# Sliding-window attention with an MLP block: three-engine W1 casts, PV heads in another order, paced casts and respaced tail steps

## Chip, cores, metric

The kernel runs on one core of one Trainium2 chip. The metric is the device time of one launch in microseconds (us); lower is better. A profiled execution has a time of its own, and inside it a span from the first to the last instruction; all places in time below are counted from the start of that span.

## What is computed

Causal attention with a window of 64 keys, 8 batches of 8 heads, 576 tokens, head size 64; the heads side by side are x, which goes through a layer norm and a two-layer MLP with ReLU, and is added to its result. Inputs and output are float32.

```python
scores = (1 / sqrt(64)) * q @ k.T
mask = (rel >= 0) & (rel < 64)          # rel = query position - key position
attn = softmax(where(mask, scores, -1e9))
x = attn @ v                            # (8, 576, 512)
xn = (x - mean(x)) / sqrt(var(x) + 1e-6) * g_ln
out = x + relu(xn @ w_ch1) @ w_ch2      # 512 -> 2048 -> 512
```

## The kernel before, in words

**Groups and periods.** The 8 x 576 token rows are cut into nine groups of 512 rows: group g below 8 holds tokens 0 to 511 of batch g, group 8 holds the last 64 tokens ("tails") of all eight batches. The loop `for g in range(NGRP)` (L639) runs the MLP of group g as a list of units of TensorE work (`mlp_units`, L400), and between the units it places the attention of the next group: `at(i, f, ...)` puts a step in the slot behind unit i. I call the stretch of one g "period g". Everything is written out in this order by hand; each engine then takes its own instructions strictly in that order and waits on semaphores, so a step that waits holds up all that stands behind it on its engine.

**Attention of a batch.** Its tokens are four blocks of 128 queries (kb or j from 0 to 3; a block is two windows of 64). `load_qk`, `load_v` (L73, L140) issue loads on SP's queue. `cast_q`, `cast_v` (L123, L149) make float16 of them on GpSimd (POOL). For batches 0 to 3 `t_main` (L217) transposes q and k on TensorE (PE) and copies from PSUM to `qkT` on ScalarE (ACT) or VectorE (DVE); later batches use DMA transposes. `vA` holds v by blocks and `vB` the same shifted by 64 tokens; for batches 0 and 1 `vB` is cast piece by piece (`vB_cur`, `vB_prev`, L161, L164), later `make_vB` (L167) makes it by two DMAs that POOL issues. `v32`, the float32 v, has one buffer, so batch b+1's v load waits for all readers of batch b's. `s_mm` (L253) is the scores and their exponentials on ACT (two instructions, even heads first, then odd ones), `s_mask` (L291) multiplies by the mask on DVE (batches 0 and 1 have the mask added on PE instead), `b_step` (L298) is attn @ v ("PV") per head on PE, then on DVE the division by the sum (`rcp`, `xn`) and the statistics; `r_step` (L325) is 1/std on ACT, `z_step` (L334) normalizes on DVE, `zt_step` (L350) transposes on PE and copies to `zT` on ACT. `bz(i, ...)` puts b_step, r_step and z_step in slots i, i+1, i+2.

**MLP.** Layer 1 is 16 column blocks of the 2048 hidden units, each four matmuls of 512 rows (`l1`, L405) or, in period 0 in part and in period 1 throughout, of two halves of 256 rows (`l1_half`, L435); ACT applies ReLU into `hrT`. Period 0 has a plain layer 2: `l2_two` (L448) for the first two blocks, `l2` (L416) for the others, and `add_out` (L427) adds on DVE into `osb1` (two buffers) and sends a store on POOL's queue. From period 1 on layer 2 is a Strassen-Winograd scheme of seven half-size products (`product`, L465, 14 units; `post`, L489, adds them up on DVE), with sums of `hrT` made on DVE in every period (`presum`, L390) and differences of W2 made once (`t_weights`, L373, eight DVE instructions over all; tiles `tw`, and one kind in `w2s` itself). The PSUM pool of layer 1 and of `l2` has two banks, so a unit waits for the sum of the tile two before it.

**Weights.** W1 comes in eight loads of 512 KB, the last four into the space of `w2s`; a load i holds two 128-row chunks c. `w1_cast` (L187) scales chunk c by g_ln and casts: c = 0 on POOL, all eight ahead of batch 1's casts, c = 1 on ACT, each at a place of its own. `rest_of_loads` (L616) then issues, in slot 6 of period 0, W2's casts and later loads, the second half of batch 1's loads and casts, and batch 2's q and k loads.

**Pacing.** POOL casts compete in time with DVE. `pace(t)` (L347) is a one-column POOL copy of a tile: it does nothing but make POOL wait for that tile, and so places the cast behind it. In the kernel before only batches 4 and later and the tails are paced.

**Tails.** `TAILS` (L629) gives the slots of periods 6 and 7 for the tail group's loads, casts, scores (first argument 8 for s_mm, then the block), masks, PV and transposes. `keep_clock(n)` (L563) issues n matmuls of no use to keep PE's clock up at the start.

Of the kernel before, what the change touches and what calls it, by code (L numbers as in the profile page):

```python
# [18 lines left out]
def kernel(  # L19
# [141 lines left out]
    def vB_cur(b, c, eng):  # L161
        evac(eng, vB[b][64:128, c, :, 0:D], v32[b][0:64, c])
# [21 lines left out]
            .rearrange("(c p) n -> p c n", p=128),  # L184
        )

    def w1_cast(i, c):  # L187
        q2, pr = divmod(i, 2)
        t = wst[("w1", i)]
        kc = 2 * pr + c  # L190
        dst = w1g[:, kc, (HID // 4) * q2:(HID // 4) * (q2 + 1)]
        if c == 0:
            nc.gpsimd.tensor_scalar(out=dst, in0=t[:, c], scalar1=g4[:, kc:kc + 1], scalar2=None, op0=ALU.mult)
        else:
            nc.scalar.activation(out=dst, in_=t[:, c], func=AF.Identity, bias=0.0, scale=g4[:, kc:kc + 1])

    def w2_load(i):
        t = p_wst.tile([128, 2, DM], FP32, tag="wld", name=f"w2s_{i}")
# [99 lines left out]
    def b_step(g, kb):  # L298
        kblk = f"{g}_{kb}"
        if kb % 2 == 0:  # L300
            x_norm[(g, kb // 2)] = p_xn.tile([128, 2, H, D], FP32, tag="xn", name=f"xn_{kblk}")
        xn = x_norm[(g, kb // 2)][:, kb % 2]
        xps = ps_x.tile([128, H, 128], FP32, tag="xps", name=f"xps_{kblk}")
        pt = pts.pop((g, kb))
        for h in range(H):
            par, hp = h % 2, h // 2
            for r in range(2):
                if g == NGRP - 1:
                    rhs = vT[kb][:, r, h, :]
                else:  # L310
                    rhs = (vA if r else vB)[g][:, kb, h, :]
                nc.tensor.matmul(out=xps[64 * r:64 * r + 64, h, :D + 1], lhsT=pt[:, par, hp, r, :], rhs=rhs,  # L312
                                 start=True, stop=True)
        rcp = p_blk.tile([128, H], FP32, tag="rcp", name=f"rcp_{kblk}")
        nc.vector.reciprocal(out=rcp, in_=xps[:, :, D])  # L315
        rcp_b = bass.AP(tensor=rcp.tensor, offset=rcp[:, :].offset,
                        ap=[rcp[:, :].ap[0], rcp[:, :].ap[1], [0, D]])
        nc.vector.tensor_tensor(out=xn, in0=xps[:, :, 0:D], in1=rcp_b, op=ALU.mult)  # L318
        stats = p_blk.tile([128, nc.vector.BN_STATS_DIM], FP32, tag="stats", name=f"stats_{kblk}")
        nc.vector.bn_stats(out=stats, in_=xn.rearrange("p h d -> p (h d)"))  # L320
        mv = p_blk.tile([128, 2], FP32, tag="mv", name=f"mv_{kblk}", bufs=5)
        nc.vector.bn_aggr(out=mv, in_=stats)  # L322
        mvs[(g, kb)] = mv
# [76 lines left out]
    def mlp_units(g, split=0, two=False):  # L400
# [64 lines left out]
        def product(n, t):  # L465
            bank, first = {1: ("X", 1), 2: ("Y", 1), 6: ("X", 0), 5: ("Z", 1), 7: ("X", 0), 3: ("Z", 0), 4: ("X", 0)}[n]
            if first and t == 0:
                pool, tag = (ps_t, "tp") if bank == "X" else (ps_mm, "mm")
                xyz[bank] = pool.tile([128, 2, 256], FP32, tag=tag, name=f"w{bank}_{g}")
            w1, w2 = slice(0, 8), slice(8, 16)  # L470
            for hc in range(8):
                tok = slice(128 * t, 128 * t + 128)
                tok2 = slice(256 + 128 * t, 256 + 128 * t + 128)
                lhsT = {1: lambda: hrT[:, hc, tok], 2: lambda: hrT[:, 8 + hc, tok], 3: lambda: sw[4][:, hc, tok],
                        4: lambda: hrT[:, 8 + hc, tok2], 5: lambda: sw[1][:, hc, tok],
                        6: lambda: sw[2][:, hc, tok], 7: lambda: sw[3][:, hc, tok]}[n]()
                rhs = {1: lambda: w2s[:, hc, lo], 2: lambda: w2s[:, 8 + hc, lo], 3: lambda: w2s[:, 8 + hc, hi],
                       4: lambda: tw[4][:, hc], 5: lambda: tw[1][:, hc], 6: lambda: tw[2][:, hc],
                       7: lambda: w2s[:, hc, hi]}[n]()
                nc.tensor.matmul(out=xyz[bank][:, t], lhsT=lhsT, rhs=rhs, start=bool(first and t == 0 and hc == 0),  # L480
                                 stop=(t == 1 and hc == 7), skip_group_check=True)
            if last and n == 4:
                post(n, slice(t, t + 1))
            elif t == 1:
                post(n, slice(0, 2))

        last = g == NGRP - 1
# [67 lines left out]
    cast_qk(0, 1)  # L555
    cast_v(0, 2, 3)
    cast_v(0, 3, 4)
    for i in range(8):
        w1_cast(i, 0)

    warm = ps_mm.tile([128, 512], FP32, tag="mm", name="warm")

    def keep_clock(n):  # L563
        m = mbias[:, :]
        mb = bass.AP(tensor=m.tensor, offset=m.offset, ap=[m.ap[0], [0, 8], m.ap[1]])
        for _ in range(n):
            nc.tensor.matmul(out=warm[:, :].rearrange("p (a i) -> p a i", i=64), lhsT=ident16, rhs=mb,
                             start=True, stop=True)


    keep_clock(4)
    keep_clock(1)
    t_main(0, 0, 0)
    keep_clock(2)
    t_main(0, 1, 0)
# [17 lines left out]
    z_step(0, 1)  # L593
    keep_clock(2)
    vB_prev(0, 2, 0)
    w1_cast(0, 1)
    s_mm(0, 2, True)
    zt_step(0, 0)
    b_step(0, 2)
    z_step(0, 2)  # L600
    zt_step(0, 1)
    w1_cast(1, 1)
    vB_cur(0, 3, 0)
    s_mm(0, 3, True)
    w1_cast(2, 1)
    w1_cast(3, 1)


    load_qk(1, 0)
# [6 lines left out]
    def rest_of_loads():  # L616
        for i in range(8):
# [9 lines left out]
        load_qk(2, 1)  # L627

    TAILS = {  # L629
        6: ((0, load_tail, 0), (3, cast_tail, 0), (7, x_tail, 0), (11, s_mm, 8, 0), (12, s_mask, 8, 0),  # L630
            (17, b_step, 8, 0), (23, zt_step, 8, 0),
            (9, load_tail, 1), (12, cast_tail, 1), (16, x_tail, 1), (20, load_tail, 2), (24, cast_tail, 2),
            (28, x_tail, 2)),
        7: ((0, s_mm, 8, 1), (1, s_mask, 8, 1), (6, b_step, 8, 1), (12, zt_step, 8, 1),
# [4 lines left out]
    for g in range(NGRP):  # L639
# [12 lines left out]
        if g == 0:  # L652
            at(0, b_step, 0, 3)
            at(0, z_step, 0, 3)
            for j in range(4):
                at(3 + j, w1_cast, 4 + j, 1)
                at(10 + j, r_step, 0, j)
            at(6, rest_of_loads)
            at(1, zt_step, 0, 2)
            at(3, zt_step, 0, 3)  # L660
            at(11, t_main, 1, 0, 0, 1)
            at(12, t_main, 1, 1, 0, 1)
            at(13, vB_cur, 1, 0, 1)
            at(13, vB_prev, 1, 0, 1)
            at(13, vB_cur, 1, 1, 1)
            at(13, vB_prev, 1, 1, 1)
            at(16, s_mm, 1, 0, True)
            at(17, s_mm, 1, 1, True)
            bz(18, 1, 0)
            bz(21, 1, 1)  # L670
            at(22, zt_step, 1, 0)
            at(24, zt_step, 1, 1)
            at(26, t_main, 1, 0, 1, 0)
            at(27, t_main, 1, 1, 1, 1)
            at(28, vB_cur, 1, 2, 0)
            at(28, vB_prev, 1, 2, 1)
            at(29, vB_cur, 1, 3, 0)
            at(29, s_mm, 1, 2, True)
            at(30, s_mm, 1, 3, True)
            at(30, load_v, 2, 0, 4)  # L680
            at(30, cast_qk, 2, 0)
            at(30, cast_qk, 2, 1)
            bz(31, 1, 2)
        if g == 1:
            at(0, alloc_qkT, 2)
            bz(1, 1, 3)
            at(2, zt_step, 1, 2)
            at(5, zt_step, 1, 3)
            at(4, alloc_v, 2)
            at(4, alloc_vB, 2)  # L690
            at(5, cast_v, 2, 0, 4)
            at(5, make_vB, 2)
            at(2, t_main, 2, 0, 0, 1)
            at(3, t_main, 2, 1, 0, 0)
            at(4, t_main, 2, 0, 1, 1)
            at(6, t_main, 2, 1, 1, 0)
            at(18, t_main, 3, 0, 0, 0)
            at(20, t_main, 3, 1, 0, 0)
            at(24, t_main, 3, 0, 1, 0)
            at(26, t_main, 3, 1, 1, 0)  # L700
            for j in range(4):
                at(9 + 4 * j, s_mm, 2, j)
                at(10 + 4 * j, s_mask, 2, j)
                bz(13 + 4 * j, 2, j)
                at(17 + 4 * j, zt_step, 2, j)
        if g > 0:
            if g == 1:
                for n, i in enumerate((1, 2, 4, 3)):
                    for c in range(2):
                        at(1 + 2 * n + c, t_weights, i, c)  # L710
            for u, i, c in ((10, 3, 0), (12, 3, 1), (14, 1, 0), (14, 2, 0), (15, 4, 0), (16, 1, 1), (17, 2, 1), (18, 4, 1)) if g == 1 else (
                    (6, 3, 0), (10, 3, 1), (12, 1, 0), (13, 2, 0), (14, 4, 0), (16, 1, 1), (17, 2, 1), (18, 4, 1)):
                at(u, presum, g, i, c)
# [19 lines left out]
        if 0 < g and b + 1 < B:  # L733
# [3 lines left out]
            at(e + 1, load_qk, n, 1)  # L737
            at(e + 4, load_v, n, 0, 4)
            if n < NPE:
                at(e + 8, cast_qk, n, 0)  # L740
                at(e + 8, alloc_qkT, n)
                at(e + 10, cast_qk, n, 1)
                at(e + 16, alloc_v, n)
                at(e + 16, cast_v, n, 0, 4)
                at(e + 16, alloc_vB, n)
                at(e + 16, make_vB, n)
            else:
                at(3, alloc_qkT, n)
                for u, x, half in ((3, 0, 0), (5, 1, 0), (8, 0, 1), (10, 1, 1)):
# [48 lines left out]
```

The softmax here doesn't subtract the row's maximum and nothing guards it: scores larger than these inputs give would overflow.

## Time and profile before

| | us |
|---|---|
| median of 4 runs | 330.19 |
| lowest and highest | 328.62, 331.68 |
| profiled execution | 330.18 |
| its span | 328.5 |
| PE busy in the span | 302.6 |
| DVE, ACT, POOL busy | 204.1, 174.9, 128.0 |

The matmuls of layer 1 start at these times, by period:

| period | 0 | 1 | 2 | 3 | 4 | 5 | 6 | 7 | 8 |
|---|---|---|---|---|---|---|---|---|---|
| start, us | 21.62 | 62.96 | 107.66 | 138.74 | 169.71 | 200.68 | 231.65 | 266.58 | 296.62 |

How to read the lines of a profile: a timeline line is start, duration, engine, line of the kernel, operation, output tile <- input tiles, shape, count, and in square brackets the idle time of the engine before it and what ended that. Names such as `qkT` or `tw` leave out buffer numbers. A busy PE includes the drain of its last matmul, so the lengths of neighbouring groups overlap a little. PEclk is the share of TensorE's full clock that was granted. DMA share is the mean busy share of the 16 DMA engines; it passes 1 where packets overlap.

### The profile page before, as it was taken

How to read it: one execution, taken by the hardware profiler on the slowest of the kernel's cores; microseconds unless marked ns; L12 is line 12 of the kernel's file. 1: busy time of each engine (PE TensorE's matmuls, PEld its weight loads, DVE VectorE, ACT ScalarE, POOL GpSimd, SP SyncE). 2: the span in 40 equal slices, each digit the busy share in tenths (PEclk: the TensorE clock that was granted, in tenths of full speed). 3: DMA queues.
4: the chain of work that ended last, by engine and by line, in shares of the span. 5: the costliest groups of instructions: out<-in, count | busy, mean ns of one | idle time of the engine just before them, and what ended most of it. 6: DMA issues, size and time to landing. Idle time of an engine off the chain costs nothing.

```text
span 328.5 us, 7565 instructions
## 1 busy us (share of the span) xinstructions
PE 302.6 (92%) x3093; PEld 199.6 (61%) x3093; DVE 204.1 (62%) x359; ACT 174.9 (53%) x348; POOL 128.0 (39%) x198
## 2 busy tenths in 40 slices
PE   4977998986999999999999999999988999999993
PEld 1546444475778448845874686468545864684582
DVE  0662455598797278737855793588378935961451
ACT  1498844364664684288337625761676347515600
POOL 6579654565400442444254334623435224001000
PEclk9999999997999999999999999999999999999998
DMA  7999999799990379696949697950996996003004
GB/s 178 269 388 266 357 291 281 184 313 212 250 196 14 128 82 228 128 278 115 253 97 268 101 239 161 217 113 2 250 190 135 153 214 161 2 2 128 0 2 128
DMA packets 120018, 57.29 MB, mean 174 GB/s; under 512 B 96112, under 2 KB 113008, under 8 KB 119984
## 3 DMA queue, kind: packets, MB, share of 16 engines
q1 hardware_dynamic: 115904, 45.10, 62.4%
q0 software_dynamic: 3104, 11.19, 10.9%
q10 hardware_dynamic: 976, 0.53, 0.6%
q8 instruction: 24, 0.39, 0.5%
q14 instruction: 10, 0.08, 0.1%
HBM read 38.80 MB, written 9.44 MB: 147 GB/s over the span
## 4 chain that ended last, share of the span: by engine, by line
PE 72%; ACT 11%; DVE 11%; issue 2%; DMA 1%; POOL 0%; DVEq 0%
PE hps L408 28%; PE wX L480 15%; PE wZ L480 8%; PE sc L279 3%; PE wY L480 3%; PE xps L312 3%; PE hph L440 3%; ACT pt L289 2%; PE ch L420 2%; PE ztp L356 2%; ACT hrT L412 2%; DVE stats L320 2%; PE tp L221 2%; DVE xn L318 2%; DVE z L342 2%
## 5 line engine op out<-in xcount | busy, mean ns | idle before, releaser
L408 PE MATMUL hps<-zT,w1g 128*128 128x512 f16 x480 | 112.3, 379 | 1.9 <-ACT zT L359 0.7
L412 ACT ACTIVATE hrT<-hps 128x512 f16<-128x512 f32 x120 | 71.3, 597 | 32.1 <-PE hps L408 29.7
L408 PEld LDWEIGHTS <-w1g 128*128 128x128 f16 x480 | 44.9, 97 | 54.7 <-issue 7.3
L480 PEld LDWEIGHTS <-sw 128*128 128x128 f16 x512 | 49.2, 98 | 6.4 <-DVE sw L398 0.6
L359 ACT COPY zT<-ztp 128x512 f16<-128x512 f16 x36 | 21.0, 585 | 43.3 <-PE ztp L356 43.3
L480 PEld LDWEIGHTS <-hrT 128*128 128x128 f16 x384 | 36.7, 98 | 6.6 <-issue 0.7
L398 DVE TENSOR_TENSOR sw<-hrT 128x1024 f16<-128x1024 f16 x32 | 21.8, 683 | 21.5 <-ACT hrT L412 21.5
L369 POOL DMA_DIRECT2D out_dram<-osb x18 | 12.6, 698 | 52.8 <-DVE osb L497 46.6
L296 DVE TENSOR_TENSOR pt<-pt,mask 128x1024 f16<-128x1024 f16 x28 | 19.7, 705 | 15.0 <-ACT pt L289 7.7
L131 POOL CAST qk<-qk 128x1024 f16<-128x1024 f32 x24 | 25.4, 1069 | 8.0 <-DMA qk<-in_k_dram 3.5
L440 PE MATMUL hph<-zT,w1g 128*128 128x256 f16 x192 | 24.7, 280 | 2.5 <-ACT zT L359 1.5
L289 ACT ACTIVATE pt<-sc 128x512 f16<-128x512 f32 x40 | 21.7, 595 | 9.3 <-PE sc L279 8.4
L320 DVE BATCH_NORM_STATS2 stats<-xn 128x6 f32<-128x512 f32 x36 | 25.0, 695 | 1.2
L318 DVE TENSOR_TENSOR xn<-xps,rcp 128x512 f32<-128x512 f32 x36 | 24.9, 692 | 1.2
L331 ACT ACTIVATE rs<-mv,epst 128x1 f32<-128x1 f32 x36 | 10.7, 296 | 27.1 <-DVE mv L322 25.9
L315 DVE RECIPROCAL rcp<-xps 128x8 f32<-128x8 f32 x36 | 7.4, 205 | 28.1 <-PE xps L312 28.1
L497 DVE TENSOR_TENSOR osb<-wX,xn 128x512 f32<-128x512 f32 (+1 forms) x25 | 16.7, 667 | 12.9 <-PE wX L480 12.9
L348 POOL CAST tok<-hrT 128x1 f32<-128x1 f16 x25 | 10.4, 416 | 34.5 <-ACT hrT L412 30.2
L150 POOL CAST vA<-v 128x512 f16<-128x512 f32 (+1 forms) x26 | 20.0, 770 | 9.0 <-DMA v<-in_v_dram 9.0
L440 PEld LDWEIGHTS <-w1g 128*128 128x128 f16 x192 | 18.6, 100 | 6.4 <-issue 3.0
L215 DVE COPY qkT<-tp 128x1024 f16<-128x1024 f16 x6 | 7.3, 1221 | 21.3 <-PE tp L221 21.3
L342 DVE TENSOR_SCALAR z<-xn,mv,rs 128x512 f16<-128x512 f32 x32 | 20.0, 629 | 0.8 <-ACT rs L332 0.6
(76 smaller groups left out, 456.6 us busy)
## 6 DMA issues: line engine op xcount, KB each, us to landing
qk<-in_q_dram SPq DMA_DIRECT2D x16, 512.0 KB, 6.6
v<-in_v_dram SPq DMA_DIRECT2D x32, 256.0 KB, 6.9
out_dram<-osb POOLq DMA_DIRECT2D x14, 512.0 KB, 6.9
w2s<-in_moe_w_ch_dram SPq DMA_DIRECT2D x12, 512.0 KB, 5.8
qk<-in_k_dram SPq DMA_DIRECT2D x8, 512.0 KB, 7.1
qk<-in_k_dram SPq DMA_DIRECT2D x16, 256.0 KB, 6.0
w1s<-in_moe_w_ch_dram SPq DMA_DIRECT2D x4, 512.0 KB, 6.7
tk<-in_k_dram SPq DMA_DIRECT2D x8, 256.0 KB, 5.2
```

Source lines behind the costliest of these rows:

```text
L131: nc.gpsimd.tensor_copy(out=dst[:, :].rearrange("p (a j) e d -> p a e j d", j=j), in_=t[:, :].rearrange("p (a e j d) -> p a e j d", e=2, j ...
L150: nc.gpsimd.tensor_copy(out=vA[b][:, c0:c1, :, 0:D], in_=v32[b][:, c0:c1])
L289: nc.scalar.activation(out=pt[:, par], in_=sc[par], func=AF.Exp, bias=0.0, scale=scale)
L318: nc.vector.tensor_tensor(out=xn, in0=xps[:, :, 0:D], in1=rcp_b, op=ALU.mult)
L320: nc.vector.bn_stats(out=stats, in_=xn.rearrange("p h d -> p (h d)"))
L342: nc.vector.tensor_scalar(out=z, in0=x, scalar1=mv[:, 0:1], scalar2=rss[(g, kb)][:, 0:1], op0=ALU.subtract, op1=ALU.mult)
L359: nc.scalar.copy(out=dst, in_=ztp)
L398: nc.vector.tensor_tensor(out=S[i], in0=a, in1=b, op=op)
L408: nc.tensor.matmul(out=hps, lhsT=w1g[:, kc, 128 * hc:128 * (hc + 1)], rhs=zT[g][:, kc, :], start=(kc == KCS[0]), stop=(kc == KCS[-1]),)
L412: nc.scalar.activation(out=hrT[:, hc, :], in_=hps, func=AF.Relu, bias=0.0, scale=1.0)
L440: nc.tensor.matmul(out=hps[:, e], lhsT=w1g[:, kc, 128 * hc:128 * (hc + 1)], rhs=zT[g][:, kc, 256 * half:256 * half + 256], start=(kc == KC ...
L480: nc.tensor.matmul(out=xyz[bank][:, t], lhsT=lhsT, rhs=rhs, start=bool(first and t == 0 and hc == 0), stop=(t == 1 and hc == 7), skip_grou ...
```

## The change

- **W1 casts.** `w1_cast` takes an engine and a column range. POOL keeps chunk 0 of loads 0 to 3 (load 1 in two halves), DVE takes chunk 0 of loads 4 to 7 in slots 3 to 6 of period 0, ACT keeps chunk 1 of all loads, at other places: the casts of loads 2 and 3 stand behind unit 0, and in slots 3 to 6 the ACT casts stand behind `zt_step` of the same slot. `vB_cur(0, 3)` goes from ACT to DVE. `rest_of_loads` goes from slot 6 to 7.
- **PV heads.** `b_step` takes the heads 0, 2, 4, 6, 1, 3, 5, 7, in all groups.
- **Warm-up.** Nine instead of five warm-up matmuls at the start.
- **Batch 2.** Its four q and k casts go from slot 30 of period 0, together, to slots 21, 22, 27 and 29, the k casts behind a pace. POOL's order becomes: cast q, pace, cast k, store 0, store 1, cast q, store 2, pace, cast k, store 3; before, it was the stores 0 to 2, the four casts, store 3. v is cast in four pieces in slots 5 to 8 of period 1, and make_vB goes from slot 5 to 8.
- **t_weights.** Kinds 1 and 2 (four instructions) go to slots 25 to 28 of period 0, kinds 4 and 3 to slots 5 to 8 of period 1, behind DVE's second copy of `qkT`.
- **Period 1.** Scores, mask and PV of batch 2 come one slot earlier, the transposes `zt_step` in slots 18, 22, 25, 28 instead of 17, 21, 25, 29. Batch 3's casts, before in slots 11, 13 and 19, unpaced, get a pace each and lie in slots 9 to 15 (q, k) and 19 to 26 (v, in pieces).
- **Tails.** Tail block 0's scores, mask, PV and transpose in period 6 go from slots 11, 12, 17, 23 to 14, 15, 20, 26.
- **Last product.** In the last period product 4 is added up and stored once for both row blocks, not for each.

```diff
@@ -186,3 +186,3 @@
 
-    def w1_cast(i, c):
+    def w1_cast(i, c, eng, lo=0, hi=512):
         q2, pr = divmod(i, 2)
@@ -190,7 +190,7 @@
         kc = 2 * pr + c
-        dst = w1g[:, kc, (HID // 4) * q2:(HID // 4) * (q2 + 1)]
-        if c == 0:
-            nc.gpsimd.tensor_scalar(out=dst, in0=t[:, c], scalar1=g4[:, kc:kc + 1], scalar2=None, op0=ALU.mult)
+        dst = w1g[:, kc, (HID // 4) * q2 + lo:(HID // 4) * q2 + hi]
+        if eng is nc.scalar:
+            eng.activation(out=dst, in_=t[:, c, lo:hi], func=AF.Identity, bias=0.0, scale=g4[:, kc:kc + 1])
         else:
-            nc.scalar.activation(out=dst, in_=t[:, c], func=AF.Identity, bias=0.0, scale=g4[:, kc:kc + 1])
+            eng.tensor_scalar(out=dst, in0=t[:, c, lo:hi], scalar1=g4[:, kc:kc + 1], scalar2=None, op0=ALU.mult)
 
@@ -304,3 +304,3 @@
         pt = pts.pop((g, kb))
-        for h in range(H):
+        for h in (0, 2, 4, 6, 1, 3, 5, 7):
             par, hp = h % 2, h // 2
@@ -481,5 +481,3 @@
                                  stop=(t == 1 and hc == 7), skip_group_check=True)
-            if last and n == 4:
-                post(n, slice(t, t + 1))
-            elif t == 1:
+            if t == 1:
                 post(n, slice(0, 2))
@@ -557,4 +555,7 @@
     cast_v(0, 3, 4)
-    for i in range(8):
-        w1_cast(i, 0)
+    w1_cast(0, 0, nc.gpsimd)
+    w1_cast(1, 0, nc.gpsimd, 0, 256)
+    w1_cast(1, 0, nc.gpsimd, 256, 512)
+    w1_cast(2, 0, nc.gpsimd)
+    w1_cast(3, 0, nc.gpsimd)
 
@@ -570,4 +571,3 @@
 
-    keep_clock(4)
-    keep_clock(1)
+    keep_clock(9)
     t_main(0, 0, 0)
@@ -595,5 +595,6 @@
     vB_prev(0, 2, 0)
-    w1_cast(0, 1)
+    vB_cur(0, 3, 1)
     s_mm(0, 2, True)
     zt_step(0, 0)
+    w1_cast(0, 1, nc.scalar)
     b_step(0, 2)
@@ -601,7 +602,4 @@
     zt_step(0, 1)
-    w1_cast(1, 1)
-    vB_cur(0, 3, 0)
+    w1_cast(1, 1, nc.scalar)
     s_mm(0, 3, True)
-    w1_cast(2, 1)
-    w1_cast(3, 1)
 
@@ -629,4 +627,4 @@
     TAILS = {
-        6: ((0, load_tail, 0), (3, cast_tail, 0), (7, x_tail, 0), (11, s_mm, 8, 0), (12, s_mask, 8, 0),
-            (17, b_step, 8, 0), (23, zt_step, 8, 0),
+        6: ((0, load_tail, 0), (3, cast_tail, 0), (7, x_tail, 0), (14, s_mm, 8, 0), (15, s_mask, 8, 0),
+            (20, b_step, 8, 0), (26, zt_step, 8, 0),
             (9, load_tail, 1), (12, cast_tail, 1), (16, x_tail, 1), (20, load_tail, 2), (24, cast_tail, 2),
@@ -654,8 +652,11 @@
             at(0, z_step, 0, 3)
-            for j in range(4):
-                at(3 + j, w1_cast, 4 + j, 1)
-                at(10 + j, r_step, 0, j)
-            at(6, rest_of_loads)
+            at(0, w1_cast, 2, 1, nc.scalar)
+            at(0, w1_cast, 3, 1, nc.scalar)
+            at(7, rest_of_loads)
             at(1, zt_step, 0, 2)
             at(3, zt_step, 0, 3)
+            for j in range(4):
+                at(3 + j, w1_cast, 4 + j, 0, nc.vector)
+                at(3 + j, w1_cast, 4 + j, 1, nc.scalar)
+                at(10 + j, r_step, 0, j)
             at(11, t_main, 1, 0, 0, 1)
@@ -680,5 +681,11 @@
             at(30, load_v, 2, 0, 4)
-            at(30, cast_qk, 2, 0)
-            at(30, cast_qk, 2, 1)
             bz(31, 1, 2)
+            at(21, cast_q, 2, 0, 0)
+            at(22, lambda: pace(zT[1][:, 0, 0:1]))
+            at(22, cast_q, 2, 1, 0)
+            at(27, cast_q, 2, 0, 1)
+            at(29, lambda: pace(qkT[1][1][:, 0, 320:321]))
+            at(29, cast_q, 2, 1, 1)
+            for u, i, c in ((25, 1, 0), (25, 1, 1), (26, 2, 0), (28, 2, 1)):
+                at(u, t_weights, i, c)
         if g == 1:
@@ -690,4 +697,5 @@
             at(4, alloc_vB, 2)
-            at(5, cast_v, 2, 0, 4)
-            at(5, make_vB, 2)
+            for c in range(4):
+                at(5 + c, cast_v, 2, c, c + 1)
+            at(8, make_vB, 2)
             at(2, t_main, 2, 0, 0, 1)
@@ -701,11 +709,10 @@
             for j in range(4):
-                at(9 + 4 * j, s_mm, 2, j)
-                at(10 + 4 * j, s_mask, 2, j)
-                bz(13 + 4 * j, 2, j)
-                at(17 + 4 * j, zt_step, 2, j)
+                at(8 + 4 * j, s_mm, 2, j)
+                at(9 + 4 * j, s_mask, 2, j)
+                bz(12 + 4 * j, 2, j)
+                at((18, 22, 25, 28)[j], zt_step, 2, j)
         if g > 0:
             if g == 1:
-                for n, i in enumerate((1, 2, 4, 3)):
-                    for c in range(2):
-                        at(1 + 2 * n + c, t_weights, i, c)
+                for u, i, c in ((5, 4, 0), (6, 4, 1), (7, 3, 0), (8, 3, 1)):
+                    at(u, t_weights, i, c)
             for u, i, c in ((10, 3, 0), (12, 3, 1), (14, 1, 0), (14, 2, 0), (15, 4, 0), (16, 1, 1), (17, 2, 1), (18, 4, 1)) if g == 1 else (
@@ -739,9 +746,13 @@
             if n < NPE:
-                at(e + 8, cast_qk, n, 0)
-                at(e + 8, alloc_qkT, n)
-                at(e + 10, cast_qk, n, 1)
-                at(e + 16, alloc_v, n)
-                at(e + 16, cast_v, n, 0, 4)
-                at(e + 16, alloc_vB, n)
-                at(e + 16, make_vB, n)
+                at(10, alloc_qkT, n)
+                for u, x, half in ((9, 0, 0), (11, 1, 0), (13, 0, 1), (15, 1, 1)):
+                    at(u, lambda u=u: pace(hrTs[g][:, 2 * (u - 8), 256:257]))
+                    at(u, cast_q, n, x, half)
+                at(19, alloc_v, n)
+                at(19, alloc_vB, n)
+                for u, c, j in ((19, 0, 0), (22, 1, 2), (23, 2, 1), (26, 3, 3)):
+                    at(u, (lambda j=j: pace(zT[b][:, 0, 128 * j:128 * j + 1])) if c % 2 == 0 else
+                       (lambda j=j: pace(rss[(b, j)])))
+                    at(u, cast_v, n, c, c + 1)
+                at(26, make_vB, n)
             else:
```

## The prediction

> **What bounds the kernel now.** I read the page's totals first, then busy time by period, then the list of waits, then the timelines of DVE and POOL around the waits that end in an idle PE.
>
> ```profile
> span 328.5 us, 7565 instructions
> PE 302.6 (92%) x3093; PEld 199.6 (61%) x3093; DVE 204.1 (62%) x359; ACT 174.9 (53%) x348; POOL 128.0 (39%) x198
> ```
>
> PE is the bound on average: 25.9 us of idle PE is nearly all that an edit without fewer matmuls can win. Busy time by period (columns: stretch, its length, then busy us of PE, PEld, DVE, ACT, POOL, granted clock, DMA share, GB/s):
>
> ```profile
> 21.60:63.00 41.40, 37.64 (x351) 20.91 (x346) 18.44 (x31) 25.73 (x53) 27.12 (x27) 1.00 0.95 288
> 63.00:107.70 44.70, 37.98 (x474) 31.53 (x473) 38.05 (x59) 25.50 (x48) 17.20 (x21) 0.96 0.92 197
> 107.70:138.70 31.00, 30.88 (x321) 20.39 (x321) 20.23 (x38) 17.32 (x36) 12.62 (x23) 1.00 0.65 135
> 231.60:266.60 35.00, 32.19 (x358) 21.38 (x356) 24.51 (x45) 19.49 (x41) 13.10 (x22) 1.00 0.87 183
> ```
>
> Periods 2 to 5 (the third line stands for them) leave PE 0.1 us each: nothing can be won there. Period 0 idles 3.8 us and runs with DMA at 0.95; period 1 idles 6.7 us with DVE busy 38 of 44.7 us; period 6 idles 2.8 us. So the places are 0, 1 and 6, and the end.
>
> **Period 1.** DVE, then POOL, in order of time (start, duration, what, idle before it and what ended that):
>
> ```profile
> 60.20 0.75 DVE L429 SCALAR_TENSOR_TENSOR osb<-ch,rs,xn 128x512 f32<-128x512 f32 x1 [2.51 <-DMA out_dram<-osb]
> ...
> 68.29 0.69 DVE L386 TENSOR_TENSOR tw<-w2s 128x1024 f16<-128x1024 f16 x1
> 68.90 1.22 DVE L215 COPY qkT<-tp 128x1024 f16<-128x1024 f16 x1
> 70.03 2.19 DVE L386 TENSOR_TENSOR tw<-w2s 128x1024 f16<-128x1024 f16 x1
> 72.14 0.58 DVE L342 TENSOR_SCALAR z<-xn,mv,rs 128x512 f16<-128x512 f32 x1
> 72.65 2.94 DVE L386 TENSOR_TENSOR tw<-w2s,tw 128x1024 f16<-128x1024 f16 x1
> 75.51 1.21 DVE L215 COPY qkT<-tp 128x1024 f16<-128x1024 f16 x1
> ```
>
> ```profile
> 53.16 0.62 POOL L150 CAST vA<-v 128x512 f16<-128x512 f32 x1 [0.21 <-DMA v<-in_v_dram]
> 56.02 1.31 POOL L369 DMA_DIRECT2D out_dram<-osb  x2 [2.24 <-issue]
> ...
> 69.78 1.89 POOL L150 CAST vA<-v 128x2048 f16<-128x2048 f32 x1 [2.35 <-DMA v<-in_v_dram]
> ...
> 73.01 2.02 POOL L131 CAST qk<-qk 128x1024 f16<-128x1024 f32 x2
> ```
>
> The weight difference `tw` takes 0.69 us alone and 2.19 and 2.94 beside a POOL cast. The copy of `qkT` at 75.51 stands behind it, and PE waits for that copy ("PE tp L221 <- DVE qkT L215: 2.7" in the waits). The clock follows (stretches as above):
>
> ```profile
> 74.00:76.00 2.00, 0.06 (x1) 0.00 (x0) 2.00 (x2) 0.60 (x1) 2.00 (x4) 1.00 1.20 301
> 76.00:78.00 2.00, 1.22 (x10) 1.10 (x10) 2.00 (x4) 0.17 (x1) 0.63 (x2) 0.55 1.06 209
> 78.00:80.00 2.00, 2.00 (x14) 1.48 (x12) 2.00 (x3) 1.31 (x2) 1.61 (x2) 0.60 1.32 187
> ```
>
> After 2.72 us without a matmul the granted clock is 0.55 to 0.60, and 24 layer-1 matmuls take 3.57 us where 24 at full clock take 2.61 (8 in 0.87): 1.0 us. The Trainium skill ("TensorE: Matmul & The Clock Gate", part 1) puts the fall at an idle window of about 3.4 us; by that rule a gap under 3 us is free, by this row it costs 1.0. I take the row, because the change makes such gaps of its own.
>
> **The change, part by part.**
>
> *W1 casts, PV head order, warm-up (period 0).* POOL loses four casts of 1.56 us (6.2 us) and gets one split in two (no row of 256 columns; 1.56 to 1.9 us for the pair). DVE gets four; nearest row `z` at L340, 0.49 to 0.56 us, in a DVE that is idle from 27.0 to 37.6. ACT keeps eight, but `vB_cur(0,3)` (0.62) leaves it, zT(0,3) no longer stands behind w1_cast(4,1) (0.61), and hrT of unit 0 goes ahead of two casts. Following ACT in order, the exponentials of block 3 start near 21.2 instead of 22.83 and unit 4 at 27.2 instead of 29.34; the first full-width layer-1 unit (33.26) comes some 2.3 us earlier. Where PE waits for exponentials, the head order leaves 8 instead of 15 or so of the matmuls behind the second one, 0.15 us twice, within the 2.3. Four more warm-up matmuls of 0.43 end at 6.3, inside PE's wait to 6.82. rest_of_loads one unit later passes no SP or POOL work. What takes the 2.3 us back is DMA: POOL's next casts wait for landings (W2, then k(1,1) at 51.17, v at 53.16), and the loads' order is unchanged. Up to there PE has 0.35 us to spare on the last W2 cast (done 47.35, needed 50.03 − 2.3). Value: 0 on the end.
>
> *Stores behind casts.* Before, POOL goes from v casts (end 53.78) to store 0 at 56.02; it lands at 60.1 (4.1 after issue) and lets DVE's third sum go at 60.20. Now the casts of q(2,0) and k(2,0) and a pace stand ahead of it. k(2,0) is issued at 50.76 and lands 5.3 later, at 56.1; cast 1.04, so 57.2. The 2.24 "issue" idle stood before the first POOL store with DVE idle too; I don't know if it is paid before the store wherever that stands. If not: issue 57.2, landing +3.4, S = 60.6. If so: issue 59.4; the third store, with DMA quiet, took 2.9: S = 62.4. Upper end with 4.1: 63.5. I take 62.4, as nothing explains the 2.24 but its being the first. Behind S on DVE stand vB (v(2)'s load on SP waits for it, and q(3), k(3), v(3) behind that), a `tw` of 0.65, the PV chain and the fourth sum, which frees the bank of unit 1. Before, unit 1 began at 64.78 = S + 4.58; now S + 4.6 = 67.0: 2.2 us later. v(2) shifts alike; its pieces are cast on landing (0.62 after the last, not 1.97), so vB of batch 2 lands at 69.7 + 2.2 + 0.7 + 8.7 = 81.3; PE wants it at 81.8. Covered by 0.5.
>
> *t_weights and the casts of batches 2 and 3.* Four of eight `tw` move to DVE's idle stretch at 53.1 to 56.5 of period 0 (about 0.65 each; v casts beside two of them), the other four behind the second copy of `qkT`. From unit 1 on: z(1,2), PV chain of (1,3), copy to +5.35, z(1,3), copy to +7.8. Unit 7 starts at +8.85, where it stood at 77.79 − 64.78 = 13.0: 4.15 us less. The new gaps ahead of units 0 and 1 (2.7 and 2.9 us) can cost clock: 0 to 0.9, I take 0.45. Then units 7 and 8 (1.74), scores (0.33), exponentials (1.08 and handover): the mask of (2,0) at 67.0 + 0.45 + 12.1 = 79.5, before 83.00.
>
> *From that mask to the end of period 1* DVE is busy 95% (9.52 of 10 us at 90 to 100), so the rest keeps its length, 107.66 − 83.00 = 24.66, less the stalls ahead of block 3's transposes and the next period's first unit (0.23 + 0.67), since zT(2,3) moves from the last unit to one before: 23.8. POOL's eight casts of batch 3 now lie in this stretch, where it was idle. The Trainium skill ("SBUF — State Buffer", section on the shared port pair) says of DVE and GpSimd that whichever starts first holds the pair for the whole instruction and "the other fully blocks". By the rule: 4 × 1.04 + 4 × 0.62 = 6.6 us at most. The row: none of the kernel's 64 presums (L398), most of them in periods paced in this way, exceeds 0.705 us (medians 0.68 to 0.69), and L342 has a median of 0.542. I take 0.4; ends 0 and 6.6. Period 2 starts at 79.5 + 23.8 + 0.4 = 103.7 instead of 107.66: −4.0. Ten more paces (0.19 to 0.73 each) lie in POOL's waits.
>
> *Tails in period 6.* Batch 7's steps hold slots 0/6/11/17; tail 0's scores shared 11, its PV 17 and its transpose 23. PE's idle there:
>
> ```profile
> 245.03 0.19 PE L279 MATMUL sc<-tqT,tkT 64*128 64x64 f16 x1 [0.68 <-ACT pt L283]
> 245.52 0.39 PE L279 MATMUL sc<-tqT,tkT 64*128 64x64 f16 x15 [0.30 <-ACT pt L283]
> 254.04 0.45 PE L312 MATMUL xps<-vt,pt 128*64 128x65 f16 x16 [1.37 <-DVE xn L318]
> 260.73 0.38 PE L356 MATMUL ztp<-ident,z 128*128 128x128 f16 x4 [0.29 <-DVE rcp L315]
> ```
>
> Sum 2.64; slots 14, 20 and 26 are free. I leave 0.3 for DVE: −2.3 (−1.5 to −2.7).
>
> *The last product* no longer stops 0.52 us for its own first half's sum, but the last sum is 0.69 instead of 0.42 and its stores are 128 KB (2.6 to 2.9 us) instead of 64 (2.8 and about 3.5): −0.2.
>
> Sum: 4.0 + 2.3 + 0.2 = 6.5. Span 328.5 − 6.5 = 322.0; with the 1.7 us around the span (330.18 − 328.5), 323.7. The profiled execution's 330.18 is the median's 330.19, so no further shift.
>
> **Rivals.** (a) *Store 0 later still.* Period 1 wins nothing once S reaches 66.4. For: one queue holds cast, pace and store. Against: every landing ahead of it is known. Left: the tails and the end, 330.2 − 2.5 = 327.7. Chance 20%. (b) *Casts collide with DVE, slower.* In the DVE-bound stretch each of the eight casts costs 1.5 us as `tw` did (2.19 − 0.69): 12.0, so 323.7 − 0.4 + 12.0 = 335.3. Below 4.6 collisions it is still a gain; beyond 6.8 it is slower by over 1%. For: those two rows. Against: the 64 presums. 10%. (c) *The 2.24 isn't paid* (S = 60.6, −1.8), no clock loss (−0.45), no collision (−0.4), tails in full (−0.3): 320.7. 10%. (d) The W1 part doing nothing is in my forecast already: it only feeds waits for DMA.
>
> **How the numbers follow.** The forecast has 60%: 323.7, its own ends 320.7 and, with S = 63.5, 0.9 of clock, 2 of collisions and 1.5 of tails, 327.5; nearly all of it lies under 326.9. Faster by over 1% (about what a measurement of this kernel can tell from no change): 60 + 10 = 0.70; within 1%: case (a), 0.20; slower: (b), 0.10. The range 320.2 to 329.0 holds (a) and most of (c) and leaves out (b).
>
> **What would show it.** Store 0 issued on POOL near 59.4 and DVE's third sum near 62.4 (under 60.6, or over 66, refutes the chain); unit 1 near 67.0; no `tw` over 1 us and no wait of PE for `qkT`; the mask of (2,0) near 79.5, period 2 near 103.7; periods 2 to 5 still 31.0; period 6 at 32.3 to 32.7. The prediction is wrong if the presums of period 1 grow beyond 0.7, if period 0's earlier PE pulls the loads forward, or if vB of batch 2 lands after PE wants it.

## The result, and the profile after

The changed kernel takes 327.83 us (median of 37 runs, 325.76 to 331.14) beside 330.85 for the kernel before on the same chips (56 runs, 327.72 to 335.47). The ratio is 0.9925, 95% interval 0.9906 to 0.9945: by the ratio 2.5 us faster where 6.5 were forecast. Single executions over 1.5% above the fastest of their kernel are left out of the ratios and of the means below. The profiled execution took 327.91 us, with these totals on its page:

```profile
span 326.2 us, 7591 instructions
PE 303.4 (93%) x3097; PEld 200.0 (61%) x3097; DVE 203.7 (62%) x363; ACT 173.5 (53%) x347; POOL 127.5 (39%) x211
```

The busy times are those of before, within 1.4 us; the span is 2.3 us shorter, and the idle of PE fell from 25.9 to 22.8 us. Where, the same stretches as before tell (period 0, 1, 2, 6; columns as in the prediction):

```profile
20.50:62.80 42.30, 37.66 (x345) 20.73 (x345) 22.12 (x36) 25.16 (x52) 25.34 (x26) 1.00 0.93 287
62.80:107.60 44.80, 38.61 (x473) 32.51 (x473) 32.87 (x57) 25.06 (x48) 19.79 (x35) 0.92 0.70 165
107.60:138.60 31.00, 30.83 (x322) 20.32 (x321) 20.91 (x39) 17.32 (x36) 12.91 (x24) 1.00 0.87 188
231.40:264.30 32.90, 31.92 (x358) 21.02 (x357) 25.35 (x45) 19.05 (x41) 12.90 (x22) 1.00 0.89 182
```

Period 1 begins at 62.78 and period 2 at 107.52: 0.14 us earlier than before, not 4.0. DVE lost 5 us of busy time there (38.05 to 32.87) and PE gained nothing; the granted clock fell from 0.96 to 0.92. Period 6 is 32.90 instead of 34.93 (−2.03). Period 7 gave 0.41 back (PE waits 0.65 for `tkT`), and the last stretch is 0.52 shorter. Sum: −2.3.

The first half of period 1 went as forecast. POOL's stores, and the sum on DVE that waits for the first of them:

```profile
55.74 1.04 POOL L131 CAST qk<-qk 128x1024 f16<-128x1024 f32 x1
59.36 1.31 POOL L369 DMA_DIRECT2D out_dram<-osb  x2 [2.57 <-issue]
```

```profile
61.97 0.75 DVE L429 SCALAR_TENSOR_TENSOR osb<-ch,rs,xn 128x512 f32<-128x512 f32 x1 [4.87 <-DMA out_dram<-osb]
...
79.59 0.69 DVE L296 TENSOR_TENSOR pt<-pt,mask 128x1024 f16<-128x1024 f16 x1 [2.14 <-ACT pt L289]
...
84.79 0.69 DVE L296 TENSOR_TENSOR pt<-pt,mask 128x1024 f16<-128x1024 f16 x1
85.39 1.26 DVE L342 TENSOR_SCALAR z<-xn,mv,rs 128x512 f16<-128x512 f32 x1
86.58 0.68 DVE L398 TENSOR_TENSOR sw<-hrT 128x1024 f16<-128x1024 f16 x1
87.29 1.41 DVE L398 TENSOR_TENSOR sw<-sw,hrT 128x1024 f16<-128x1024 f16 x1
...
91.03 0.18 DVE L322 BATCH_NORM_AGGREGATE mv<-stats 128x2 f32<-128x6 f32 x1
```

The last five lines are where it broke. `z` takes 1.26 us and a sum of the presums 1.41, where their neighbours take 0.54 and 0.69. Two paced casts of batch 3 lie exactly there on POOL, themselves stretched from 1.04 to 1.51 us:

```profile
84.86 1.51 POOL L131 CAST qk<-qk 128x1024 f16<-128x1024 f32 x1
86.33 0.37 POOL L348 CAST tok<-hrT 128x1 f32<-128x1 f16 x1
86.64 1.51 POOL L131 CAST qk<-qk 128x1024 f16<-128x1024 f32 x1
```

So the variance of block 1 (`mv`) ends some 1.4 us later than it does without these two delays (the kernel without paces, below), and on ACT the step behind it stands ahead of a copy that PE waits for:

```profile
91.25 0.29 ACT L331 ACTIVATE rs<-mv,epst 128x1 f32<-128x1 f32 x1 [3.10 <-DVE mv L322]
91.57 0.20 ACT L332 ACTIVATE rs<-rs 128x1 f32<-128x1 f32 x1
91.68 0.99 ACT L213 COPY qkT<-tp 128x1024 f16<-128x1024 f16 x1
```

```profile
92.73 0.38 PE L356 MATMUL ztp<-ident,z 128*128 128x128 f16 x4 [3.40 <-ACT qkT L213]
92.95 1.57 PE L480 MATMUL wY<-w2s,hrT 128*128 128x256 f16 x8
94.32 1.91 PE L480 MATMUL wX<-tw,sw 128*128 128x256 f16 x8
```

PE idles 3.40 us, and then groups of eight matmuls (x8) take 1.57 and 1.91 us where the same eight take 1.04 at 87.85. The clock by stretch of 2 us says the same, for this gap and for the 2.58 us ahead of unit 1 at 66.40:

```profile
66.00:68.00 2.00, 1.60 (x8) 0.99 (x7) 0.84 (x2) 0.71 (x3) 1.36 (x4) 0.50 1.33 243
...
94.00:96.00 2.00, 2.00 (x11) 1.36 (x10) 1.25 (x3) 0.00 (x0) 1.25 (x2) 0.50 0.04 8
```

### The profile page after: what moved, and what is told of

The parts are those of the page before. It is cut to its first block, busy times and chain, and to the rows that moved or that the text cites. A ratio compares the mean times of both kernels' runs of the same rounds, so it can differ in the third digit from the quotient of the medians.

```text
span 326.2 us, 7591 instructions
## 1 busy us (share of the span) xinstructions
PE 303.4 (93%) x3097; PEld 200.0 (61%) x3097; DVE 203.7 (62%) x363; ACT 173.5 (53%) x347; POOL 127.5 (39%) x211
## 3 DMA queue, kind: packets, MB, share of 16 engines
q1 hardware_dynamic: 115888, 45.10, 62.4%
## 4 chain that ended last, share of the span: by engine, by line
PE 70%; DVE 9%; ACT 7%; DMA 4%; SPq 3%; issue 2%; POOL 2%; DVEq 0%
PE hps L408 28%; PE wX L480 16%; PE wZ L480 8%; PE hph L440 4%; PE wY L480 4%; PE xps L312 3%; PE sc L279 3%; DMA w1s<-in_moe_w_ch_dram 2%; POOL w1g L195 2%; SPq L144 2%; ACT hrT L412 2%; DVE stats L320 2%; DVE xn L318 2%; PE ztp L356 2%; PE tp L221 2%
## 5 line engine op out<-in xcount | busy, mean ns | idle before, releaser
L131 POOL CAST qk<-qk 128x1024 f16<-128x1024 f32 x24 | 26.4, 1100 | 11.6 <-DMA qk<-in_q_dram 7.6
L348 POOL CAST tok<-hrT 128x1 f32<-128x1 f16 x29 | 11.8, 408 | 40.2 <-ACT hrT L412 30.5
L495 DVE TENSOR_TENSOR osb<-wX,xn 128x512 f32<-128x512 f32 x24 | 16.4, 685 | 12.6 <-PE wX L480 12.6
L150 POOL CAST vA<-v 128x512 f16<-128x512 f32 x32 | 21.1, 663 | 3.0 <-DMA v<-in_v_dram 2.9
L342 DVE TENSOR_SCALAR z<-xn,mv,rs 128x512 f16<-128x512 f32 x32 | 20.5, 642 | 0.8 <-ACT rs L332 0.6
L348 POOL CAST tok<-zT 128x1 f32<-128x1 f16 x12 | 3.9, 326 | 37.7 <-ACT zT L359 37.7
```

What stands on the lines that cost most here:

```text
L131: nc.gpsimd.tensor_copy(out=dst[:, :].rearrange("p (a j) e d -> p a e j d", j=j), in_=t[:, :].rearrange("p (a e j d) -> p a e j d", e=2, j ...
L150: nc.gpsimd.tensor_copy(out=vA[b][:, c0:c1, :, 0:D], in_=v32[b][:, c0:c1])
L342: nc.vector.tensor_scalar(out=z, in0=x, scalar1=mv[:, 0:1], scalar2=rss[(g, kb)][:, 0:1], op0=ALU.subtract, op1=ALU.mult)
```

## The experiments

Theory A: the order on ACT (copy of `qkT` behind 1/std) costs the time. Theory B: DVE is late anyway. From the second set on, theory C: two DVE operations that collide with paced casts make the gap long, and the half clock behind it costs as much again. All kernels are timed against the kernel before on the same chip (median there 329.53, 331.19 and 331.27 us in the three sets).

**First set.** The copy one slot earlier:

```diff
-            at(18, t_main, 3, 0, 0, 0)
+            at(17, t_main, 3, 0, 0, 0)
```

> The changed kernel with one step moved: the transposes of batch 3's first q half stand in slot 17 instead of 18, so that ACT's copy of them is ahead of the 1/std of block (2,1) again, as it was before the change. Theory A (the order on ACT is the cause): PE's 3.40 us wait ahead of the transpose of (2,0) and the half clock behind it (about 1.4 us) go; period 2 starts near 102.7 instead of 107.5, time 323. Theory B (DVE is late anyway, since the PV chain of (2,1) and the mask of (2,2) now stand ahead of the presum that product 6 needs, and two DVE operations are held up by POOL casts): PE does some 1.5 us of work and then waits for that presum near 93.6; time 326.3 to 327.

Measured: 326.56 us, ratio 0.9927 (0.9892 to 0.9962), not distinguishable from the changed kernel. The wait for `qkT` is gone, and PE waits in other words: 0.23 us for DVE, then 1.63 for `osb` (L495) and 0.61 for `sw`, with the clock again at 0.76 from 93 to 100. From the mask of (2,0) to period 2 it takes 27.11 us instead of 27.93, so 0.8 of the 4.8 us that A had promised. The order on ACT alone isn't the cause; A falls.

The casts of batch 3 without pace:

```diff
                 for u, x, half in ((9, 0, 0), (11, 1, 0), (13, 0, 1), (15, 1, 1)):
-                    at(u, lambda u=u: pace(hrTs[g][:, 2 * (u - 8), 256:257]))
                     at(u, cast_q, n, x, half)
```

> The changed kernel without the four paces ahead of batch 3's q and k casts; the casts keep their place in POOL's order and run when their data land, near 73 to 78. Theory A: no change of the wait for ACT; within 0.5 us of the changed kernel. Theory B: z(2,0) falls from 1.26 to 0.54 us and the presum at 87.29 from 1.41 to 0.69, so block (2,1)'s chain ends 1.4 us earlier; but the W2 differences at 75 to 77.5 meet the casts and may lose 1 to 3 us. Time between 326 and 329.

Measured: 324.58 us, ratio 0.9853 (0.9809 to 0.9897), about 2.4 us less than the changed kernel. Both theories had the time wrong, but B had `z` and the sum right. POOL now casts at 72.2, 73.7, 75.3 and 80.3, when the loads land, and `z` and the sums keep their times. What B feared is there too: the last four weight differences take 3.7 instead of 2.6 us beside these casts. Up to the mask it costs nothing, as DVE's wait for the exponentials ahead of the mask shrinks from 2.14 to 1.00 us:

```profile
84.78 0.54 DVE L342 TENSOR_SCALAR z<-xn,mv,rs 128x512 f16<-128x512 f32 x1
85.24 0.68 DVE L398 TENSOR_TENSOR sw<-hrT 128x1024 f16<-128x1024 f16 x1
85.96 0.69 DVE L398 TENSOR_TENSOR sw<-sw,hrT 128x1024 f16<-128x1024 f16 x1
```

PE's gap is 1.44 us shorter, and the clock stays up behind it:

```profile
90.68 0.38 PE L356 MATMUL ztp<-ident,z 128*128 128x128 f16 x4 [1.96 <-ACT qkT L213]
```

```profile
93.00:100.00 7.00, 7.00 (x113) 6.17 (x111) 5.90 (x12) 4.21 (x8) 2.14 (x5) 1.00 0.00 0
```

Period 2 begins at 103.81.

Batch 2's scores, masks, PV and transposes back in their slots of before (9, 10, 13 and 17, each + 4j):

> The changed kernel with batch 2's scores, masks, PV and transposes in the slots of before (9, 10, 13 and 17, each plus 4 per block). Both theories see PV (2,1) behind the presums and the copy ahead of 1/std again. Theory A: 323, all of the 4.8 us back. Theory B: the presum of product 6 ends 2 us earlier against the mask, but each step comes 0.9 us later and the stalls at the end of the period (0.67 and 0.23) come back: 325 to 326.

Measured: 326.94 us, ratio 0.9925 (0.9893 to 0.9956). The mask comes at 80.75 and period 2 25.36 us later, at 106.11: the 3.40 us gap is gone (longest wait behind the mask 1.1 us, for `z`), the clock is 1.00 from 79 to 107, and `z` still takes 1.25. That is 2.57 us less from mask to period 2 than in the changed kernel, but the mask comes 1.16 later, and by the ratio the time is that of the changed kernel, above what A and B gave. So this one settles little.

Stores 0 and 1 ahead of batch 2's casts, and no pace between those:

```diff
-            at(21, cast_q, 2, 0, 0)
-            at(22, lambda: pace(zT[1][:, 0, 0:1]))
-            at(22, cast_q, 2, 1, 0)
+            at(25, cast_q, 2, 0, 0)
+            at(25, cast_q, 2, 1, 0)
```

> The changed kernel with batch 2's first q and k casts in slot 25, behind the first two stores, and without the pace between them. The store is issued near 56.0 instead of 59.4 and lands near 60.1, so DVE's third sum starts at 60.2 instead of 61.97 and unit 1 of period 1 at 64.7 instead of 66.40. If what follows is a chain (DVE's work from the mask of (2,0) on), all 1.7 us reach the end: 326.1. If the ACT order hides it (the wait for 1/std ends by DVE's own chain, which also moves), the same. If vB of batch 2 or batch 3's casts bind instead, less than 0.7.

Measured: 324.78 us, ratio 0.9877 (0.9826 to 0.9929). The store goes at 52.92, directly behind the cast of v, with no unexplained idle ahead of it; the third sum runs at 58.90, and unit 1 at 63.53 behind a gap of 0.78 us instead of 2.58. The mask comes at 75.69. By the ratio that is 1.6 us less than the changed kernel, near the 1.7 expected. But PE's 3.40 us gap is there as in the changed kernel, and this time the clock stays at 0.50 for longer, so that period 2 begins only at 104.65.

**Second set.** Both edits that paid, together:

> The casts of q(2,0) and k(2,0) stand behind stores 0 and 1 (without the pace between them), and the casts of batch 3 have no pace. Theory C (two operations of DVE that are held up beside paced casts, 1.44 us, make a gap on PE long enough for the half clock; each of the two edits pays by itself): mask of (2,0) near 75.2, then 24.8 us as in the kernel without paces, period 2 at 99.9 to 101, granted clock 1.00 from 86 to 100, time 320.5 to 322.0. Rival D (both edits win the same microseconds, since the loads of batch 3 or DVE are next in line): 324.0 to 324.8.

Measured: 323.06 us, ratio 0.9789 (0.9734 to 0.9844). Period 2 begins at 101.21, 24.84 us after the mask of (2,0) (76.37, 1.2 later than expected), with the clock at 1.00 throughout. The edits add in the profile; the median is 1 us above what C gave, below what D gave.

The same with the copy one slot earlier:

> As the kernel with both edits, and the copy of qkT of batch 3 one slot earlier, ahead of 1/std on ACT. Theory A' (with DVE no longer held up, the 2.0 us for which PE waits for that copy are set by ACT's order): 1 to 2 us less than the kernel with both edits. Theory B (DVE's sum that product 6 needs is just as late, the wait gets another name): within 0.5 of it.

Measured: 322.20 us, ratio 0.9745 (0.9697 to 0.9794), the fastest of all kernels here; 0.9 below the one without the earlier copy, just short of A' and above B, with intervals that overlap. From mask to period 2 it takes 24.24 instead of 24.84 us: of the 1.96 us that PE waited for the copy, 0.6 were the order's own. Its profiled execution is the slowest of its six and has the 2.58 us gap ahead of unit 1 back, the third sum running only at 61.75.

Only the first two of the four paces left out:

```diff
-                    at(u, lambda u=u: pace(hrTs[g][:, 2 * (u - 8), 256:257]))
+                    if half or g != 1:
+                        at(u, lambda u=u: pace(hrTs[g][:, 2 * (u - 8), 256:257]))
```

> Of the four paces ahead of batch 3's casts the first two are left out, those ahead of the third and fourth cast stay. Theory C: the casts that DVE collides with are the third and fourth (84.86 and 86.64 in the changed kernel), which stay where they are, so z takes 1.26 and the sum 1.41 again, PE idles 3.4 and period 2 begins at 107 to 107.7: 327.3 to 328.0. Rival E (what paid in the kernel without paces was that the casts as such came earlier, by the staging buffers and loads that they free, or that POOL had less to do): at least half of its 3.2 us stay, 324.6 to 326.2.

Measured: 327.09 us, ratio 0.9899 (0.9849 to 0.9949). The third and fourth cast run at 84.31 and 86.09 for 1.51 us each, `z` takes 1.26, the sum 1.41, and the gap is 3.40. So the collision is with these two casts, as C says, and E falls: by the ratio, the time is within 0.9 us of the changed kernel's and above E's range, though just under C's. But in the profiled execution (324.79 us, the fastest of its six) the clock did not fall behind the gap:

```profile
92.17 0.38 PE L356 MATMUL ztp<-ident,z 128*128 128x128 f16 x4 [3.40 <-ACT qkT L213]
```

```profile
93.00:100.00 7.00, 7.00 (x112) 6.20 (x110) 6.12 (x12) 3.46 (x8) 3.32 (x6) 1.00 0.01 3
```

The steps of tail 0 back in slots 11, 12, 17 and 23:

> Tail 0's steps in period 6 back in slots 11, 12, 17 and 23, all else as changed. If period 6's 2.0 us come from the slots alone: periods up to 6 unchanged, period 6 at 34.6 to 35.2 instead of 32.9, the idle before PV of (7,1) (1.37) back, time 329.5 to 330.2. If they come from something else in the change (DVE or ACT in another phase): period 6 under 34 and under 328.8.

Measured: 330.57 us, ratio 1.0005 (0.9964 to 1.0047). Period 6 is 34.91 us, with the idle of before in the list of PE's waits (us in total, times, longest):

```profile
PE xps L312 <- DVE xn L318: 1.4, 1, 1.4
PE sc L279 <- ACT pt L283: 1.0, 2, 0.7
```

The periods ahead were expected unchanged and weren't: period 2 begins 1.5 us later than in the changed kernel, 1.0 of it in the stretch where the clock falls behind the gap (below).

**Third set.** The kernel before with the W1 part alone:

> The kernel before with the W1 part alone (casts on three engines, head order of PV, warm-up, loads one unit later). If period 0 is set by landings, as forecast: its first layer-1 unit comes near 20.6 instead of 21.6, period 1 begins at 62.6 to 63.2 all the same, and the time is that of before within 0.5. Rival: the 1.1 us are carried to the end, 329.5 or less beside 330.6.

Measured: 328.85 us, ratio 0.9942 (0.9901 to 0.9982). In the profile its first layer-1 unit comes at 20.60 and period 1 at 61.77, 1.2 us earlier than before; PE then waits 1.16 us for `osb` and 1.09 for `zT`, and period 2 begins at 107.14, 0.5 earlier. The interval puts it 0.6 to 3.3 us below the kernel before, more than the 0.5 us that I allowed, so the first expectation isn't met. The last table below tells where this lies: its length at full clock is that of the kernel before (324.7 and 324.8 us in this set), and the clock took 1.9 ± 0.7 instead of 3.9 ± 0.6.

The kernel before with the tails' slots alone:

> The kernel before with tail 0's steps in slots 14, 15, 20 and 26 of period 6, nothing else. If the tails' gain is the slots' own and adds to the rest: period 6 at 32.7 to 33.1 instead of 34.9, all ahead of it as before, time 1.7 to 2.1 under before. Rival: it needs the other parts (another phase of DVE): under 1.0 less.

Measured: 328.35 us, ratio 0.9930 (0.9883 to 0.9976). Period 6 is 32.83 us. The tails' 2.1 us are the slots' own. That all ahead stays as before did not come true: period 2 began 2.3 us earlier (see the end).

The changed kernel with twelve idle matmuls in the gap:

```diff
             at(18, t_main, 3, 0, 0, 0)
+            at(18, lambda: keep_clock(12, ps_mm.tile([128, 512], FP32, tag="mm", name="fill")))
```

> The changed kernel with twelve matmuls of 512 columns into a spare PSUM buffer ahead of the transposes of z(2,0), inside the 3.40 us in which PE waits for the copy of qkT (12 x 0.213 = 2.56 us; nothing reads them). Theory C, clock term: the gap shrinks to under 1 us, DVE and ACT keep their times up to there (mask of (2,0) near 79.6, the copy at 91.7), the granted clock stays 1.00 from 93 to 100, period 2 begins 1.5 to 3 us earlier than 107.5, and span times granted clock stays at 321.8 while the clock lost falls from 4.2 to about 3; time 326.0 to 327.0. Rival: the matmuls behind the gap are slow for another reason (they wait for DVE's sums): no gain, or slower by what the twelve cost.

Measured: 327.68 us, ratio 0.9896 (0.9820 to 0.9973). In the profile it does what C says: `z` takes 1.26 and the sum 1.41 as in the changed kernel, PE idles 0.80 instead of 3.40 us, the clock is 1.00 from 93 to 100, and period 2 begins at 106.13:

```profile
89.44 2.75 PE L568 MATMUL fill<-mbias,ident 128*128 128x512 f16 x12
93.00 0.38 PE L356 MATMUL ztp<-ident,z 128*128 128x128 f16 x4 [0.80 <-ACT qkT L213]
```

By the ratio it is 1.0 us under the changed kernel, by the median 0.15, and the intervals overlap: over many runs the gain of 1.4 us is not shown.

**The stages side by side**, from the profiles (us). The third stage ends with PE's wait for the copy, the fourth with the first matmul of period 2:

| kernel | unit 1 at | to mask (2,0) | to the gap's end | to period 2 | period 2 at |
|---|---|---|---|---|---|
| changed | 66.40 | 13.19 | 13.14 | 14.79 | 107.52 |
| no pace | 65.81 | 13.17 | 11.70 | 13.13 | 103.81 |
| stores first | 63.53 | 12.16 | 13.13 | 15.83 | 104.65 |
| both | 64.22 | 12.15 | 11.71 | 13.13 | 101.21 |
| half the paces | 65.87 | 13.17 | 13.13 | 13.14 | 105.31 |
| tails back | 66.87 | 13.15 | 13.14 | 15.83 | 108.99 |
| filled gap | 66.83 | 13.03 | 13.14 | 13.13 | 106.13 |

The three other variants of the changed kernel (copy first, slots back, both with copy first) have no long wait for that copy. The three stages take only two or three values each. The second stage is 13.0 to 13.2 with the 2.58 us gap ahead of unit 1 and 12.15 without: 1.0. The third is 13.14 with the two collisions and 11.70 without: 1.44. The fourth is 13.13 where the clock holds, 14.79 or 15.83 where it falls: 1.66 or 2.70.

**Over all runs**, span times granted clock is an estimate of the length at full clock, and span times (1 − clock) of what the clock took; it counts a low clock as a loss even where PE would have waited (means with twice their standard error; each clock is given to 0.001, or 0.3 us):

| kernel | runs | at full clock | taken by the clock |
|---|---|---|---|
| before, all three sets | 51 | 325.0 ± 0.4 | 3.3 ± 0.4 |
| changed | 36 | 321.8 ± 0.3 | 4.1 ± 0.5 |
| no pace | 5 | 320.6 ± 0.8 | 2.2 ± 0.6 |
| both | 6 | 319.2 ± 0.3 | 2.4 ± 1.4 |
| both, copy first | 6 | 318.4 ± 0.6 | 2.1 ± 0.7 |
| copy first | 12 | 320.8 ± 0.7 | 4.3 ± 0.9 |
| slots back | 10 | 321.8 ± 0.5 | 3.2 ± 0.6 |
| stores first | 6 | 319.7 ± 0.8 | 3.8 ± 1.3 |
| half the paces | 6 | 322.3 ± 0.8 | 2.9 ± 1.1 |
| filled gap | 6 | 323.0 ± 0.7 | 2.4 ± 0.9 |
| tails back | 12 | 323.1 ± 0.3 | 5.8 ± 1.0 |
| before, third set | 18 | 324.8 ± 0.6 | 3.9 ± 0.6 |
| before with W1 alone | 11 | 324.7 ± 0.4 | 1.9 ± 0.7 |
| before with tails alone | 12 | 323.2 ± 0.7 | 3.2 ± 1.1 |

The change saves 3.2 us of work and waiting and gives 0.8 back in clock. Without pace it would have saved 4.4 and the clock 1.1 as well. The filled gap has the lower clock loss that C wants, but 1.2 us more at full clock than the changed kernel, where equality was expected; why is open. So of the two terms, the collisions are shown by edits that bring them and take them away; that the lower clock behind the gap costs its 1.7 us rests on single profiled executions.

## Why the prediction was wrong

**The number.** 327.83 us lies beside the 327.7 of rival (a), but not by its mechanism: (a) needed the third sum at 66.4 or later, and it ran at 61.97. That its number fits is luck. (The upper end of my own forecast, given as 327.5, adds up to 327.7 from its parts.)

**What held.** Store 0 at 59.36 (59.4), third sum at 61.97 (62.4), unit 1 at 66.40 (67.0), no `tw` above 1.09 us (I had said 1, so by a strict reading that sign failed) and no wait for the second `qkT`, mask of (2,0) at 79.59 (79.5), and no wait of PE for `vB`. Periods 2 to 5 are unchanged, the tails gave 2.03 (2.3), the last product 0.52 (0.2). Even period 2 at 103.7 came true in the kernel without paces (103.81), in part by errors that cancel: there unit 1 was 1.2 us early, and the clock cost 0.6 more ahead of the mask than I took.

**What failed** is the step "From that mask to the end of period 1 ... keeps its length", with its collision term of 0.4. It took 27.93 us, not 24.2, and the sign that I had named came true: a presum of period 1 took 1.41 us, over the 0.7. Of the 3.7 us too many, 1.44 are the two collisions (13.14 against 11.70) and 1.66 the clock behind the gap that they lengthen (14.79 against 13.13); 0.6 is what is left with neither (24.83 without paces). That is the order on ACT, which I had not looked at: with both edits and the copy one slot earlier the stretch takes 24.24, against 24.84 without the earlier copy. The clock's share is that of this profiled execution; with half the paces the same gap was followed by no fall.

**Why the 0.4 was too small.** I took it from 64 presums of which none exceeded 0.705 us, "most of them in periods paced in this way". That row was no evidence: in periods 2 to 5 of the trace before, the casts begin at the end of a presum, none has one already running beside it, so these presums had never met what the change would bring. A presum and the cast behind it, from period 2 of the trace before:

```profile
112.53 0.69 DVE L398 TENSOR_TENSOR sw<-hrT 128x1024 f16<-128x1024 f16 x1 [1.51 <-ACT hrT L412]
113.21 1.03 POOL L131 CAST qk<-qk 128x1024 f16<-128x1024 f32 x1
```

The rows that had met it were in the same trace, behind a median: `z` (L342) has a median of 0.542, and 1.90 us at 64.67, beside casts:

```profile
61.78 3.98 POOL L131 CAST qk<-qk 128x1024 f16<-128x1024 f32 x4
64.67 1.90 DVE L342 TENSOR_SCALAR z<-xn,mv,rs 128x512 f16<-128x512 f32 x1
```

The Trainium skill's rule ("SBUF — State Buffer", section "SBUF: two separate sides"), which I set aside for the row, puts the price at the whole instruction ("the other fully blocks"): `z` 0.72 longer and the sum 0.72, both less than a cast of 1.04, fit that better than my row. Rival (b) had the mechanism, at 1.5 us of end time for each of eight casts; there were two that counted, and with the clock behind them they cost 3.1.

**The clock was left out of the step.** I priced 1.0 us for the old gap and 0 to 0.9 for the new ones, but only for those ahead of units 0 and 1; behind the mask I put it at nothing. The gap ahead of unit 1 cost 1.0. A wait that I hadn't found, on ACT's copy behind 1/std, made a third gap, harmless at 1.96 us in the two kernels that show it (1.00 behind it) and expensive at 3.40 in three of the four that have it. So DVE's 1.44 us cost PE 3.1 in the changed kernel's profile.

**W1.** With it alone the time is 0.2 to 1.0% lower, not 0. Its length at full clock is unchanged within the errors, as forecast; what is lower is the loss to the clock, by 2.0 ± 0.9 us. Why is open.

## What to carry to other kernels

A row shows that two engines don't disturb each other only where they overlap in it: before taking "none exceeded" as a bound, count how many of its instructions had the other engine running when they began, and read the maximum, not the median. Here a pace that moved casts into a stretch in which the other engine set the time was worse than no pace: without it they collided as well, but where that engine had a wait to spare. Where the traces show a clock that falls behind some of PE's waits, price a delay twice, once as the wait and once as the clock behind it.

## What the runs showed that I had not expected

- The clock's loss seems to come in portions. A fall behind a gap cost 1.0 us at unit 1 and 1.66 or 2.70 at the later place, and over 51 runs of the kernel before the loss is 1.6 to 2.0 us in 8 runs, 3.3 in 15 and 5.0 to 5.3 in 9. The other 19 lie elsewhere, six of them at 2.9, and the rounding is 0.3 us, so the portions are a guess.
- No single length of gap decides. Gaps of 2.56 to 2.72 us were followed by a fall in each of ten profiles, gaps of 3.40 in three of four. With the copy first the clock fell to 0.53 behind waits of 0.23, 1.63 and 0.61 us that follow closely, while a single wait of 1.96 was followed by no fall in two profiles. The Trainium skill ("TensorE: Matmul & The Clock Gate", part 1) speaks of an idle window of about 3.4 us; as a bound below which a gap is free, these rows contradict it.
- The idle of 2.0 to 2.8 us ahead of POOL's first store is not the price of being first: where the store stands directly behind the cast of v, there is none (four profiles). But DVE's sum behind it then starts 5.8 to 6.6 us after the issue instead of 2.6 as in the changed kernel, so that from POOL's being free to that sum it takes 4.9 to 6.6 us in all of them. What holds it isn't shown.
- The kernel before varies by itself: with only the tails' slots changed, its 2.7 us wait for `qkT` shrank to 0.46 us in the profiled execution, and period 2 began at 105.34 instead of 107.66. Part of what the change was to remove is not there in each run.
